# After the last attention head: its scaling moved to ScalarE, two additions moved to GpSimd, two filler products fewer, and the first expert's product placed earlier

## The chip, the cores and the metric

The kernel runs on one core of a Trainium2 chip. The metric is the device time of one execution in microseconds (us), of which the median over several runs counts. TensorE (PE) multiplies, VectorE (DVE) and ScalarE (ACT) work element by element and can read the accumulators in PSUM, GpSimd (POOL) works element by element on SBUF, and SyncE (SP) issues all the transfers of this kernel.

## The reference, cut to what matters

Sixteen heads of hash-bucket attention (768 positions, 64 wide) make 1536 tokens of 512 values; a soft mixture of experts and a gated feed-forward layer follow, all in float32.

```python
mask = q_bucket[:, :, :, None] == k_bucket[:, :, None, :]
scores = np.where(mask, scale * q @ k.T, -1e9)          # per head
attn = softmax(scores);  x = attn @ v                   # x: 1536 x 512, head n fills 64 columns

logits = x @ phi                                        # 1536 x 32 slots, 4 for each of 8 experts
d = softmax over tokens of logits
slot_input = d.T @ x                                    # 32 x 512
h = np.maximum(slot_input[e] @ w1[e], 0)                # w1: 8 x 512 x 1024, 16 MB
slot_out[e] = h @ w2[e]                                 # w2: 8 x 1024 x 512, 16 MB
c = softmax over slots of logits;  y = c @ slot_out     # 1536 x 512

h = y @ w_in;  out = (h * sigmoid(1.702 * h)) @ w_out   # 512 -> 2048 -> 512
```

## The kernel before, in words

**Attention.** A long string, `ATTENTION`, lists every step of the sixteen heads in the order in which each engine's queue receives them; nothing reorders them later. The score steps (`c`, `s`) make a 128 x 384 block of scores, `e` (ScalarE, line 556) takes the exponential into a tile `P`, `av` (TensorE, line 571) multiplies it with the values, and `p` (`psum_add`, line 564) adds up the six `P` tiles of a head into `Ps`, from which `sum1` gets the softmax denominators. For heads 0 to 14 the additions are on GpSimd, for head 15 on VectorE. `Ps` has two halves (`h` 0 and 1) of 384 columns; `p.15.4.1` is head 15's addition of tile 4 into half 1.

**The chain behind the last two heads.** For heads 14 and 15 TensorE sums the columns of `Ps` (line 612), VectorE transposes the sums (line 614), two small operations add the count of positions without a match (lines 628 and 631, on GpSimd for head 14 and on VectorE for head 15), and VectorE takes the reciprocal `rr` (line 633). Head 14 is then scaled by `xnorm1` (step `xg.14`, line 679): six operations of 128 x 64, each with one column of `rr`, from `nv` into the token tiles `XH`. Head 15's product is copied out of PSUM by `avo.15` (ScalarE, line 581), transposed on TensorE (`xtok.15`, line 650) and scaled by six VectorE operations (`xn1.15`, line 729). The string ends with

```
sum1.14 av.15.4 av.15.5 xg.14 avo.15 sum1.15 xtok.15 xn1.15 raw.16
```

**The slots.** Six transposes `xTp` (line 839) take the columns that heads 14 and 15 have filled, two copies into `etile` follow (line 844 on ScalarE, line 842 on VectorE), filler products `spin("t3")` on TensorE (line 203; the table `W` says how many, and their result is not used), and the last part of the logits (line 848). Then come a maximum, exponentials, transposes, and the slot inputs in two halves of 256 columns: `slots(i, t)` multiplies on TensorE (line 887), `slots1(i)` scales on VectorE (line 896), `slots2(i)` transposes on TensorE (line 903) and copies into `siT[i]` on ScalarE (line 904).

**The experts.** `expert_in` multiplies `siT` with the first-layer weights: four tiles of 1 MB to a group, of which `c` = 0 and 1 need `siT[0]`, and 2 and 3 need `siT[1]` (line 1029, result `hp`). Each tile that has been used is given back (`give`), and `more()` then issues the next transfer of the list `coming` into the free place; line 232 is the transfer of a whole 1 MB tile `w`. The list holds `w15` to `w31`, then the weights of the feed-forward layer. `etile` also occupies such a place. The second layer follows on TensorE (line 1068, result `sop`), and behind it the feed-forward layer, whose 384 large products (line 1218) fill TensorE until the end.

Of the kernel before, what the change touches and what calls it, by code (L numbers as in the profile page):

```python
# [8 lines left out]
AF = mybir.ActivationFunctionType  # L9
ALU = mybir.AluOpType  # L10
# [151 lines left out]
def build(nc, tc, qk0, qk, v, phi, consts, w1a, w1, w2, w_in, w_out, out):  # L162
# [4 lines left out]
    V = nc.vector  # L167
    A = nc.scalar
    G = nc.gpsimd
# [15 lines left out]
    def xrow():  # L185
        return XH[:, rows_of.popleft(), :]
# [2 lines left out]

    W = {'s0': 6, 's1': 2, 's2': 1, 's3': 1, 's6': 1, 's7': 3, 's8': 2, 't0': 0, 't1': 0, 't2': 0, 't3': 3, 't4': 2, 't5': 0, 't6': 0, 't7': 0, 'f0': 2, 'f1': 0, 'f2': 4, 'f3': 8, 'f4': 13}
    idle = {}
    bz = cpool.tile([128, 1], F32, name="bz")
    V.memset(LT[:, 0:128], 0.0)
# [2 lines left out]
    def spin(n):  # L198
        spins(W[n])

    def spins(n):
        for _ in range(n):
            T.matmul(idle[0], LT[:, 0:128], LT[:, 0:128], start=True, stop=True)
# [13 lines left out]
    def give(name):  # L217
        free.append(slot_of.pop(name))
# [30 lines left out]
    def piece(w, j):  # L249
        return w[j] if isinstance(w, list) else w[:, j, :]  # L250
# [80 lines left out]
    vsb, Pt, Ps, mxs, xu, rec, xTs, nvs, sms, xtp = {}, {}, {}, {}, {}, {}, {}, {}, {}, {}  # L331
# [226 lines left out]
    def psum_add(n, kt, h):  # L558
        if kt == 1 and h == 0:
            Ps[n] = pq.tile([128, S], F32, name=f"Ps{n}", tag="Ps", bufs=3)  # L560
        last = n == NH - 1
        e = V if last else G
        c = slice(h * HS, (h + 1) * HS)
        e.tensor_tensor(out=Ps[n][:, c], in0=Pt[n, 0][:, c] if kt == 1 else Ps[n][:, c], in1=Pt[n, kt][:, c], op=ALU.add)  # L564

# [86 lines left out]
    def xout(n, i):  # L652
        b, h = n // H, n % H
        return xt[b * 6 + i][:, h * D : (h + 1) * D]
# [21 lines left out]

    def xnorm1(n):
        for i in range(KT):
            G.tensor_scalar(
                out=xout(n, i), in0=nvs[n][:, i, :], scalar1=rec[n][:, i : i + 1], scalar2=None, op0=ALU.mult  # L680
            )

    def xtrans(p, hf):
        b, c = p // 4, p % 4
# [38 lines left out]
    def pool_norm(n):  # L723
        xnorm1(n)
# [16 lines left out]
    def load_phi():  # L741
# [5 lines left out]
        "code": code0, "raw": load_raw, "v": load_v, "win": load_win, "we": load_expert, "wx": lambda k: load_part(NWA, k), "phi": load_phi,  # L747
        "a0": amax0, "a": amax, "mred": mred, "mr0": mrow0, "mr1": mrow1, "mp": mprep, "mr": mrow, "ms": mstore,
        "c": cross, "s": scores, "e": power, "p": psum_add, "av": av, "avo": avout, "vs": vsum, "vs2": vsum2, "sum": sums, "rec": recs,
        "sum1": sums1, "nom": nomatch, "xtok": xtok, "xn": xnorm, "xp": xplus, "xadd": xadd1, "xg": pool_norm, "xn1": norms,  # L750
        "xT": xtrans, "lg": logits, "w1": win1, "w2": win2, "w3": win3, "w4": win4,
# [52 lines left out]
    def more():  # L804
        while coming and free and (coming[0][0] is load_expert or any(x != "wc" for x in free)):
            f, a = coming.popleft()
            f(*a)
# [10 lines left out]
    def mm(shape, name):  # L818
        return mps.tile(shape, F32, name=name, tag="mm", bufs=4)
# [29 lines left out]
    for g in range(4):  # L849
        r = slice(32 * g, 32 * g + 32)  # L850
        G.tensor_copy(
            out=R4[r, :].rearrange("p (r j) -> p r j", r=4), in_=ident[r, r].unsqueeze(1).to_broadcast([32, 4, 32])
# [13 lines left out]
    t1 = mm([128, 128], "cm1")  # L866
# [4 lines left out]
    for t in range(3):  # L871
        t3 = mm([128, 128], f"etp{t}")
# [12 lines left out]
    def slots(i, t):  # L885
        for g in range(4):
            T.matmul(
                sps[i][32 * g : 32 * g + 32, :],
                E[:, t, 32 * g : 32 * g + 32],
                xt[3 * g + t][:, i * 256 : i * 256 + 256],  # L890
                start=t == 0,
                stop=t == 2,
            )

    def slots1(i):
        V.tensor_scalar(
            out=Ssb[i], in0=sps[i], scalar1=fac, scalar2=None, op0=ALU.mult
        )

    def slots2(i):  # L900
        t5 = mm([128, 2, 32], f"sip{i}")
        for c in range(2):
            T.matmul(t5[:, c, :], Ssb[i][:, c * 128 : (c + 1) * 128], I4, start=True, stop=True)
        A.copy(out=siT[i], in_=t5)
# [3 lines left out]
    t2 = mm([128, 1], "cm2")  # L908
# [8 lines left out]
    slots2(0)  # L917
    V.tensor_reduce(out=den, in_=den3, axis=AX.X, op=ALU.add)
    V.tensor_tensor(out=den, in0=den, in1=fac, op=ALU.mult)
    slots(1, 1)  # L920
    slots(1, 2)
    slots1(1)
    t4 = mm([128, 1], "den2")
    T.matmul(t4, R4, den, start=True, stop=True)
    dn1 = col("dn1")
# [97 lines left out]
    def expert_in(g, fh, between=None):  # L1023
        hp = mps.tile([128, 512], F32, name=f"hp{g}{fh}", tag="hp", bufs=2)
        for c in range(4):
            i = (g * 2 + fh) * 4 + c
            w = wtile.pop(i)
            for j in range(4):
                T.matmul(hp[32 * j : 32 * j + 32, :], siT[c // 2][:, c % 2, :], piece(w, j), start=c == 0, stop=c == 3)
            give(f"w{i}")  # L1030
            more()
            if c == 0 and between:
                between()
        hs = xrow()
        V.tensor_scalar(
            out=hs, in0=hp, scalar1=0.0, scalar2=emr[:, g : g + 1], op0=ALU.max, op1=ALU.mult
        )
        return hs

    def expert_tr(g, fh, hs):  # L1040
        tp = mm([128, 4, 128], f"hTp{g}{fh}")
        for t in range(4):
            T.transpose(tp[:, t, :], hs[:, t * 128 : (t + 1) * 128], ident)
        hT[g, fh] = xrow().rearrange("p (t c) -> p t c", t=4)
        A.copy(out=hT[g, fh], in_=tp)

    def last_slots():
        slots2(1)
        give("etile")
        more()  # L1050

    done = []
    for g in range(2):
        for fh in range(2):
            done.append((g, fh, expert_in(g, fh, None if done else last_slots)))

            if len(done) == 3:
                expert_tr(*done[0])
                expert_tr(*done[1])
# [3 lines left out]
    for g in range(2):  # L1063
        for fc in range(8):
            i = 16 + g * 8 + fc
# [12 lines left out]
            for x in early.get(i, "").split():  # L1078
                e, f = x.split(".")
# [265 lines left out]
```

## Time and profile before

| what | value |
|---|---|
| median of 3 runs | 437.98 us (437.12 to 439.15) |
| the profiled execution | 437.46 us |
| its span in the profile | 435.5 us |
| mean granted TensorE clock | 0.999 |
| TensorE busy | 425.6 us, 98% of the span |
| VectorE, ScalarE, GpSimd busy | 303.3, 282.1, 221.5 us |
| transfers | 73.22 MB, mean 168 GB/s |

The profile is one execution; 1.96 us of its time lie outside the span. Times in the rows below count from the start of the span. A busy TensorE here is an engine that has an instruction in flight, so the 98% say little about a single stretch. Between 223 and 298 us the transfers of the expert and feed-forward weights run at 300 to 430 GB/s with one gap; from 300 us on there are next to none.

### The profile page before, as it was taken

How to read it: one execution, taken by the hardware profiler on the slowest of the kernel's cores; microseconds unless marked ns; L12 is line 12 of the kernel's file. 1: busy time of each engine (PE TensorE's matmuls, PEld its weight loads, DVE VectorE, ACT ScalarE, POOL GpSimd, SP SyncE). 2: the span in 40 equal slices, each digit the busy share in tenths (PEclk: the TensorE clock that was granted, in tenths of full speed). 3: DMA queues.
4: the chain of work that ended last, by engine and by line, in shares of the span. 5: the costliest groups of instructions: out<-in, count | busy, mean ns of one | idle time of the engine just before them, and what ended most of it. 6: DMA issues, size and time to landing. Idle time of an engine off the chain costs nothing.

```text
span 435.5 us, 8323 instructions
## 1 busy us (share of the span) xinstructions
PE 425.6 (98%) x2968; PEld 284.7 (65%) x2968; DVE 303.3 (70%) x520; ACT 282.1 (65%) x571; POOL 221.5 (51%) x258
## 2 busy tenths in 40 slices
PE   8999999999999999999999999999999999999996
PEld 6646656566666566656564333577787888888885
DVE  4788798978979899878876226578776845445441
ACT  7668887877889898877862006465776646445441
POOL 5648777888787876979973002234656310000000
PEclk9999999999999999999999999999999999999999
DMA  7454457454557453663799899994000003001001
GB/s 239 132 173 135 127 179 233 150 178 155 171 192 215 130 211 134 210 229 84 263 295 406 335 423 396 417 424 190 1 2 1 2 0 146 0 0 74 0 2 72
DMA packets 28373, 73.22 MB, mean 168 GB/s; under 512 B 4398, under 2 KB 9512, under 8 KB 24876
## 3 DMA queue, kind: packets, MB, share of 16 engines
q1 hardware_dynamic: 28332, 72.69, 47.1%
q8 instruction: 23, 0.38, 0.3%
q14 instruction: 18, 0.15, 0.1%
HBM read 64.16 MB, written 7.34 MB: 164 GB/s over the span
## 4 chain that ended last, share of the span: by engine, by line
PE 76%; DMA 8%; DVE 7%; ACT 5%; issue 1%; SPq 1%; POOL 1%; ACTq 0%; DVEq 0%; POOLq 0%
PE o L1218 30%; PE av L571 12%; PE b L542 8%; PE a L494 7%; PE b L550 7%; DMA w<-in_w 6%; PE h L1190 3%; DVE MX L501 2%; DVE QK L393 1%; SPq L398 1%; ACT QK L371 1%; DVE Ps L564 1%; PE bp L425 1%; PE sm L612 1%; PE xtp L650 1%
## 5 line engine op out<-in xcount | busy, mean ns | idle before, releaser
L564 POOL TENSOR_TENSOR Ps<-Ps,P 128x384 f32<-128x384 f32 x120 | 119.8, 1015 | 9.8 <-ACT P L556 7.4
L1218 PE MATMUL o<-wh,ring 128*128 128x512 f32 x384 | 110.2, 396 | 0.6 <-DVE cT L981 0.6
L556 ACT ACTIVATE P<-b 128x384 f32<-128x384 f32 x192 | 86.8, 488 | 23.0 <-PE b L550 20.3
L501 DVE TENSOR_REDUCE MX<-a 128x1 f32<-128x768 f32 x90 | 85.6, 951 | 19.4 <-PE a L494 18.3
L1218 PEld LDWEIGHTS o<-wh,ring 128*128 128x128 f32 x384 | 71.0, 188 | 15.7 <-issue 1.4
L571 PE MATMUL av<-P,v 128*32 128x384 f32 x768 | 75.5, 492 | 0.0
L1199 DVE TENSOR_TENSOR XH<-h,XH 128x384 f32<-128x384 f32 x64 | 35.3, 556 | 46.4 <-ACT XH L1195 46.3
L542 PE MATMUL b<-QK 128*128 128x384 f32 x192 | 66.7, 369 | 0.4 <-ACT P L556 0.2
L550 PE MATMUL b<-QK 78*128 78x384 f32 (+1 forms) x192 | 60.9, 349 | 0.3 <-ACT QK L531 0.3
L1218 PE MATMUL o<-wl,ring 128*128 128x512 f32 x192 | 55.4, 395 | 0.0
L1195 ACT ACTIVATE XH<-h 128x384 f32<-128x384 f32 x64 | 31.3, 491 | 30.1 <-PE h L1190 30.1
L494 PE MATMUL a<-QK 77*128 77x384 f32 x180 | 50.0, 359 | 0.8 <-DVE MX L501 0.2
L1204 ACT CAST ring<-XH 128x384 fp32r<-128x384 f32 x64 | 32.7, 513 | 23.3 <-DVE XH L1199 22.1
L542 PEld LDWEIGHTS b<-QK 128*128 128x128 f32 x192 | 35.5, 188 | 16.7 <-ACT P L556 8.7
L1218 PEld LDWEIGHTS o<-wl,ring 128*128 128x128 f32 x192 | 35.8, 188 | 10.6 <-issue 2.5
L550 PEld LDWEIGHTS b<-QK 78*128 78x128 f32 (+1 forms) x192 | 35.7, 189 | 6.5 <-issue 5.9
L564 POOL TENSOR_TENSOR Ps<-P,P 128x384 f32<-128x384 f32 x30 | 30.2, 1010 | 19.0 <-ACT P L556 18.9
L494 PEld LDWEIGHTS a<-QK 77*128 77x128 f32 x180 | 29.9, 189 | 13.6 <-DVE MX L501 9.2
L1019 POOL TENSOR_TENSOR wl<-XH,wh 128x512 fp32r<-128x512 f32 x16 | 22.7, 1421 | 31.0 <-ACT wh L1014 30.8
L1209 DVE TENSOR_TENSOR ring<-XH,ring 128x384 fp32r<-128x384 f32 x64 | 37.4, 588 | 1.4 <-ACT ring L1204 1.1
L571 PEld LDWEIGHTS av<-P,v 128*32 128x32 f32 x768 | 19.9, 109 | 23.8 <-issue 21.3
L393 DVE TENSOR_TENSOR QK<-raw,lo 64x384 fp32r<-64x384 f32 x56 | 30.9, 552 | 2.1 <-ACT lo L387 0.9
(171 smaller groups left out, 535.4 us busy)
## 6 DMA issues: line engine op xcount, KB each, us to landing
w<-in_w SPq DMA_DIRECT2D x17, 1024.0 KB
w<-in_w1a SPq DMA_DIRECT2D x56, 256.0 KB
wif<-in_w_in SPq DMA_DIRECT2D x16, 512.0 KB
wof<-in_w_out SPq DMA_DIRECT2D x7, 1024.0 KB
raw<-in_qk SPq DMA_DIRECT2D x15, 384.0 KB
win<-wn SPq DMA_DIRECT2D x16, 256.0 KB
v<-in_v SPq DMA_DIRECT2D x16, 192.0 KB
win<-win SPq DMA_DIRECT2D x3, 1024.0 KB
```

Source lines behind the costliest of these rows:

```text
L393: V.tensor_tensor(out=QK1[n % 2][r, s, c], in0=raw[n][r, c], in1=lot[h][r, :].bitcast(F32), op=ALU.subtract)
L494: T.matmul(a[:, h, 0:HS], q2[0:CROW + 1, 0, i * 128 : (i + 1) * 128], q2[0:CROW + 1, 1, h * HS : (h + 1) * HS], start=True, stop=True,)
L501: V.tensor_reduce(out=MX[:, n % 2, i : i + 1], in_=a[:, :, 0:HS], axis=AX.XY, op=ALU.max)
L542: T.matmul(b, q1[:, 1, kt * 128 : (kt + 1) * 128], q1[:, 0, h * HS : (h + 1) * HS], start=True, stop=False)
L550: T.matmul(b, q2[rows, 1, kt * 128 : (kt + 1) * 128], q2[rows, 0, qs], start=False, stop=True)
L556: A.activation(out=Pt[n, kt][:, h * HS : (h + 1) * HS], in_=bps[n, kt, h], func=AF.Exp, scale=0.125)
L564: e.tensor_tensor(out=Ps[n][:, c], in0=Pt[n, 0][:, c] if kt == 1 else Ps[n][:, c], in1=Pt[n, kt][:, c], op=ALU.add)
L571: T.matmul(avp[n][32 * c : 32 * c + 32, :], vt[n][:, kt, d : d + 32], Pt[n, kt][:, h * HS : (h + 1) * HS], start=kt == 0, stop=kt == KT - 1,)
L1199: V.tensor_tensor(out=gt[i], in0=hp[i], in1=gt[i], op=ALU.mult)
L1204: A.copy(out=gh[i], in_=gt[i])
L1209: (e or V).tensor_tensor(out=gl[i], in0=gt[i], in1=gh[i].bitcast(F32), op=ALU.subtract)
L1218: T.matmul(op[grp, t], u[i][:, t * 128 : (t + 1) * 128], w[wq][:, wi, :], start=f == 0 and j == 0, stop=f == NF - 1 and j == 2,)
```

## The change

It makes four edits. `xnorm1` runs its six operations on ScalarE in place of GpSimd. Of head 15's additions, `p.15.4.1` and `p.15.5.1` go to GpSimd, the other eight stay on VectorE. `spin("t3")` issues one filler product in place of three. The second half's remaining slot products (`slots(1, 1)`, `slots(1, 2)`, `slots1(1)`) leave their place ahead of the first expert and are issued from `expert_in`, behind its first weight tile; `last_slots` moves from behind the first tile to behind the second.

```diff
-    W = {..., 't3': 3, 't4': 2, ...}
+    W = {..., 't3': 1, 't4': 2, ...}
...
         last = n == NH - 1
-        e = V if last else G
+        e = V if last and (h == 0 or kt < 4) else G
...
     def xnorm1(n):
         for i in range(KT):
-            G.tensor_scalar(
-                out=xout(n, i), in0=nvs[n][:, i, :], scalar1=rec[n][:, i : i + 1], scalar2=None, op0=ALU.mult
-            )
+            A.activation(out=xout(n, i), in_=nvs[n][:, i, :], func=AF.Copy, scale=rec[n][:, i : i + 1])
...
     V.tensor_tensor(out=den, in0=den, in1=fac, op=ALU.mult)
-    slots(1, 1)
-    slots(1, 2)
-    slots1(1)
     t4 = mm([128, 1], "den2")
...
             give(f"w{i}")
             more()
-            if c == 0 and between:
-                between()
+            if c < 2 and between:
+                between[c]()
...
+    def more_slots():
+        slots(1, 1)
+        slots(1, 2)
+        slots1(1)
...
-            done.append((g, fh, expert_in(g, fh, None if done else last_slots)))
+            done.append((g, fh, expert_in(g, fh, None if done else (more_slots, last_slots))))
```

Here is ScalarE's queue at the end of attention, before the change; `P_5` are the exponentials of head 15, `xu` is the copy `avo.15`.

```order
L556 ACTIVATE P_3_3181<-b_3_1_3200 128x384
L556 ACTIVATE P_5_3164<-b_5_1_3179 128x384
L581 COPY xu_3265<-av_3212 128x384
L844 COPY etile<-xTp_3329 128x384
L864 ACTIVATE etile,den_3353<-lg,nmx 128x128 x3
```

And here is the same place after the change.

```order
L556 ACTIVATE P_3_3181<-b_3_1_3200 128x384
L556 ACTIVATE P_5_3164<-b_5_1_3179 128x384
L679 ACTIVATE XH<-nv_3193,rr_3249 128x64 x6
L581 COPY xu_3265<-av_3212 128x384
L842 COPY etile<-xTp_3329 128x384
L862 ACTIVATE etile,den_3351<-lg,nmx 128x128 x3
```

Head 14's six scalings now stand ahead of head 15's copy `xu` on the same queue. Below is one piece of the difference of GpSimd's queue at the same place; `nv` is the part of positions without a match, `rec` belongs to head 14.

```order
 L640 TENSOR_TENSOR nv_3177<-vsb_3150,nma 128x384
 L640 TENSOR_TENSOR nv_3193<-vsb_3150,nma 128x384
+L564 TENSOR_TENSOR Ps_3134<-Ps_3134,P_4_3095 128x384
+L564 TENSOR_TENSOR Ps_3134<-Ps_3134,P_5_3164 128x384
 L628 TENSOR_SCALAR rec_3246<-nma 128x6
 L631 TENSOR_TENSOR rec_3246<-sms_3244,rec_3246 128x6
-L679 TENSOR_SCALAR XH<-nv_3193,rr_3249 128x64 x6
```

The two additions stand ahead of both small operations of head 14's denominators. TensorE's queue from the first half's slot transposes (`sip`) on reads so before the change (`sps` are the slot products, `hp` the first expert's):

```order
L903 MATMUL sip_3398<-phs,etile 128x32 x2
L887 MATMUL sps_3375<-XH,etile 32x256 x8
L924 MATMUL den_3413<-den,phs 128x1
L1029 MATMUL hp_3421<-w_137,siT_3372 32x512 x4
L903 MATMUL sip_3428<-phs,etile 128x32 x2
L1029 MATMUL hp_3421<-w_325,siT_3372 32x512 x4
L1029 MATMUL hp_3421<-w_545,siT_3373 32x512 x4
```

And so after the change:

```order
L901 MATMUL sip_3396<-phs,etile 128x32 x2
L919 MATMUL den_3402<-den,phs 128x1
L1024 MATMUL hp_3410<-w_137,siT_3370 32x512 x4
L885 MATMUL sps_3373<-XH,etile 32x256 x8
L1024 MATMUL hp_3410<-w_325,siT_3370 32x512 x4
L901 MATMUL sip_3432<-phs,etile 128x32 x2
L1024 MATMUL hp_3410<-w_545,siT_3371 32x512 x4
```

The first expert's product has passed the eight slot products. The first product that reads the copy of the second half's `sip` (`siT_3373`, now `siT_3371`) had one other weight tile's products between itself and that `sip`; now it stands directly behind it.

## Rows read from the trace of the kernel before

**Rows 1.** Page, part 2: granted TensorE clock in 40 slices of the span.

```profile
PEclk9999999999999999999999999999999999999999
```

**Rows 2.** Chain that ended last, 231 to 274 us: start, length, what.

```profile
231.37 0.20 POOL rec L631
231.91 2.54 POOL XH L679 x6
234.82 0.67 PE idle L203 x6
235.49 0.88 PE lg L848 x4
...
241.78 1.00 PE sps L887 x16
...
243.09 0.99 PE hp L1029 x8
244.09 0.56 PE sip L903 x4
...
255.89 17.51 DMA w<-in_w
```

**Rows 3.** Windows: engines' busy time and instructions, clock, DMA share, GB/s.

```profile
242.00:244.00 2.00, 2.00 (x26) 0.67 (x18) 0.94 (x4) 0.03 (x1) 0.00 (x0) 1.00 0.76 311
244.00:246.00 2.00, 2.00 (x24) 1.04 (x24) 0.00 (x0) 0.21 (x1) 0.00 (x0) 1.00 0.43 98
256.00:260.00 4.00, 4.00 (x44) 1.17 (x36) 0.75 (x1) 0.00 (x0) 0.00 (x0) 1.00 1.01 426
```

**Rows 4.** Timeline of the transfer queue and of TensorE's weight loads.

```profile
244.15 0.33 SPq L232 DMA_DIRECT2D w<-in_w  x1
...
272.15 0.13 PEld L1068 LDWEIGHTS sop<-w,XH 128*32 128x32 f32 x4 [0.30 <-issue]
273.45 0.16 PEld L1068 LDWEIGHTS sop<-w,XH 128*32 128x32 f32 x8 [1.17 <-DMA w<-in_w]
```

**Rows 5.** Additions: timeline of VectorE and GpSimd, then line 564 (min/median/max ns).

```profile
224.40 1.25 DVE L564 TENSOR_TENSOR Ps<-Ps,P 128x384 f32<-128x384 f32 x1
228.25 0.54 DVE L564 TENSOR_TENSOR Ps<-Ps,P 128x384 f32<-128x384 f32 x1
...
224.03 1.21 POOL L564 TENSOR_TENSOR Ps<-Ps,P 128x384 f32<-128x384 f32 x1
...
L564 POOL TENSOR_TENSOR Ps<-Ps,P x120: 992/1010/1377, 19.9 to 224.0; 128x384 f32<-128x384 f32 x120
```

**Rows 6.** Timeline of ScalarE, then line 967.

```profile
231.22 0.48 ACT L581 COPY xu<-av 128x384 f32<-128x384 f32 x1 [3.87 <-PE av L571]
234.47 0.48 ACT L844 COPY etile<-xTp 128x384 f32<-128x384 f32 x1 [2.78 <-POOL XH L679]
236.99 0.37 ACT L864 ACTIVATE etile<-lg,nmx 128x128 f32<-128x128 f32 x1 [2.04 <-DVE nmx L856]
...
244.69 0.21 ACT L904 COPY siT<-sip 128x64 f32<-128x64 f32 x1 [2.66 <-PE sip L903]
...
L967 ACT COPY XH<-XH x8: 272/278/283, 265.8 to 267.0; 128x96 f32<-128x96 f32 x8
```

**Rows 7.** Timeline of VectorE and TensorE, 231 to 236 us.

```profile
231.61 0.19 DVE L633 RECIPROCAL rr<-rec 128x6 f32<-128x6 f32 x1 [0.39 <-POOL rec L631]
232.67 1.24 DVE L729 SCALAR_TENSOR_TENSOR XH<-xtp,rr,nv 128x64 f32<-128x64 f32 x6
234.92 0.56 DVE L842 COPY etile<-xTp 128x384 f32<-128x384 f32 x1 [1.00 <-issue]
...
231.75 0.55 PE L650 MATMUL xtp<-cst,xu 128*128 128x128 f32 x3
```

**Rows 8.** Windows behind the last product, columns as in group 3.

```profile
433.00:434.00 1.00, 0.00 (x0) 0.00 (x0) 0.00 (x0) 0.00 (x0) 0.00 (x0) 1.00 0.76 260
434.00:436.00 2.00, 0.00 (x0) 0.00 (x0) 0.00 (x0) 0.00 (x0) 0.00 (x0) 0.64 0.00 1
```

More of the change, by code (lines that the diff above doesn't have):

```diff
@@ L188, in build @@
     ones = cst[:, C_ONE : C_ONE + 32]
-    W = {'s0': 6, 's1': 2, 's2': 1, 's3': 1, 's6': 1, 's7': 3, 's8': 2, 't0': 0, 't1': 0, 't2': 0, 't3': 3, 't4': 2, 't5': 0, 't6': 0, 't7': 0, 'f0': 2, 'f1': 0, 'f2': 4, 'f3': 8, 'f4': 13}
+    W = {'s0': 6, 's1': 2, 's2': 1, 's3': 1, 's6': 1, 's7': 3, 's8': 2, 't0': 0, 't1': 0, 't2': 0, 't3': 1, 't4': 2, 't5': 0, 't6': 0, 't7': 0, 'f0': 2, 'f1': 0, 'f2': 4, 'f3': 8, 'f4': 13}
     idle = {}
```

## The prediction

> **What bounds the kernel now.** I read the page's line of the granted clock first: TensorE has its full clock in all 40 slices [rows 1], so no stretch is dear because of the clock. Then I read the chain that ended last, from the end backwards, to find what the edited stretch is worth. Behind 274 us it is TensorE's large products; ahead of that the second layer of the experts waits until 273.45 for its last weight tile [rows 4], whose transfer was issued at 255.89 [rows 2]. So the edits, all ahead of 246 us, reach the end of the kernel only through this meeting of two paths: TensorE's own work and the weight transfers.
>
> How near the two paths lie is read from TensorE's weight loads [rows 4]. They come every 0.43 us (0.30 idle and 0.13 load). Behind the one at 272.15 the next was due at 272.58 and came at 273.45. TensorE is thus only 0.87 us ahead of the transfers: a gain on the transfers alone is worth at most 0.87 us, and a delay on TensorE alone is free up to 0.87 us.
>
> The windows [rows 3] show what the transfers lack: at their full rate they move 426 GB/s, but 311 from 242 to 244 us and 98 from 244 to 246. That is 2 x (115 + 328) / 426 = 2.1 us of lost transfer time, because no place was free until the first expert's first tile had been used: its products ran from 243.09 for 0.99 us [rows 2], and the next transfer was issued at 244.15 [rows 4].
>
> What sets 243.09 is the chain behind the last heads, where I read engine by engine: reciprocal of head 14 at 231.61 on VectorE [rows 7], six scalings on GpSimd from 231.91 for 2.54 us [rows 2], transposes, filler products, logits, slots. Beside it runs head 15: copied by ScalarE at 231.22 [rows 6], transposed on TensorE at 231.75, scaled on VectorE from 232.67 for 1.24 us [rows 7], done at 233.91. GpSimd's scalings, done at 234.45, are the later of the two by 0.54 us.
>
> **Two additions on GpSimd.** VectorE loses two additions of 0.54 us, but the sums of head 14 now wait for GpSimd. Head 15's addition 3 into half 1 runs on VectorE from 228.25 for 0.54 us [rows 5]; with the hand-over of 0.11 us that is seen between the reciprocal's end (231.80) and 231.91, GpSimd starts at 228.90. Two additions at the median of 1.01 us [rows 5] end at 230.92. Only then come the two small operations of head 14 at some 0.20 us each [rows 2], and VectorE's reciprocal 0.04 us later: 231.36 against 231.61, a gain of 0.25 us. With the least duration, 0.992, it is 0.29; with the greatest, 1.377, it is a loss of 0.48.
>
> On VectorE the neighbours pay. While GpSimd's addition ran from 224.03 to 225.24, VectorE's addition of the same shape took 1.25 us and ended 0.41 us behind it; alone it took 0.54 [rows 5]. So `p.15.5.0` will end near 229.91 + 0.41 = 230.3, where three additions in a row of 0.54 us would end at 229.9. The transposition of head 14's sums follows before 231.0, when GpSimd is still at its queue: no cost beyond what is counted.
>
> This is what the Trainium skill says against such a move (GPSIMD Engine Reference, Key points): GpSimd shares its SBUF interfaces with VectorE and contends with instructions that have two SBUF inputs. This case's trace agrees (1.25 against 0.54 us); by the rule alone the two additions would be a loss for VectorE, which the sum above allows for.
>
> **Scaling on ScalarE.** The trace has no ScalarE operation of 128 x 64 whose scale is a column of a tile. The nearest are copies of 128 x 96 at 0.278 us, which start 1.2 / 7 = 0.17 us apart, and exponentials of 128 x 128 with a column operand at 0.37 [rows 6]. I take 0.31 us for one and 0.20 from start to start (the overlap of the copies, 0.11, taken off): 5 x 0.20 + 0.31 = 1.3 us for six. The ends are 5 x 0.17 + 0.27 = 1.1 us and, without any overlap, 6 x 0.37 = 2.2 us. So the six fall from 2.54 to 1.3 us.
>
> The Trainium skill prices an ACTIVATE with immediates at 186 ns plus 0.833 ns for each column, 93 more for a column operand, and lets neighbours overlap by 93 (ScalarE: Activation LUTs, What ACT_TABLE_LOAD costs). By it the six would take an estimated 5 x 0.24 + 0.33 = 1.5 us, 0.2 us more than the rows give, and the result would be 0.2 us later.
>
> But in ScalarE's queue the six stand ahead of head 15's copy, which before ran at 231.22 and so ahead of the reciprocal. That copy is what is late next, and TensorE's transposes, VectorE's six scalings and the last transposes wait behind it. Step by step: reciprocal 231.36 + 0.19 + hand-over 0.11 = 231.66; six scalings to 232.96; copy 0.48, to 233.44; transposes 0.05 later and 0.55 long, to 234.04; VectorE's six 0.05 later and 1.24 long, to 235.33. Before, the last scaling ended at 234.45. Head 15, which had 0.54 us to spare, now ends the stretch **0.88 us later** than GpSimd did. From the bounds (additions 0.992 or 1.377, scalings 1.1 or 2.2) this lies between +0.6 and +2.5 us.
>
> **Filler products.** Six records took 0.67 us [rows 2], so four records fewer are 0.45 us. They lay beside VectorE's copy, which ended at 234.92 + 0.56 = 235.48 [rows 7], while ScalarE's had ended at 234.95 [rows 6]. Without them the first half of the logits can run from about 235.0, and the second at 235.53, where before it started about halfway through the 0.88 us from 235.49 [rows 2]. I take 0.3 us of gain; the bounds are 0 and 0.45. Together the stretch ends 0.88 - 0.3 = **0.6 us later** (+0.2 to +2.5).
>
> **First expert first.** Ahead of the first tile's products 1.00 us of slot products goes away [rows 2]; the wait for the first half's copy gives some 0.05 back. The first tile is thus free 0.95 us earlier within this chain. The slot products return behind it, so TensorE's work up to the third tile is the same. But the second half's `sip` now stands directly ahead of the third tile's products, which need ScalarE's copy of it. Before, this copy (244.69, 0.21 us long [rows 6], behind the `sip` that ends at 244.65 [rows 2]) lay beside the second tile's products. Now TensorE waits: 0.04 + 0.21 + 0.05 = 0.3 us, and with the refilling of its pipeline I take 0.4 (0.3 to 0.5). A further place, that of `etile`, comes free only behind the second tile; that is 1.00 + 0.99 + 0.56 = 2.6 us behind the first, but the second tile's own place comes free 2.0 us behind the first, while one transfer of 1.05 MB at 426 GB/s still runs (2.5 us), so the queue need not run dry again.
>
> **The sum.** Transfers: 0.6 - 0.95 = 0.35 us earlier, to 273.10. TensorE: 272.58 + 0.6 + 0.4 = 273.58. The later decides: 273.6 against 273.45, so **+0.1 us**. The profiled execution took 437.46 us (span 435.5 and 1.96 around it), so 437.6 by its own time. It lies 0.5 us below the median of the runs shown; on the median's scale the forecast is 438.1 us. With all bounds (stretch +0.2 to +2.5, wait 0.3 to 0.5) the change is -0.4 to +2.1 us.
>
> **The rivals.** A measurement of this kernel tells some 0.5%, 2.2 us, from no change.
>
> *The early release counts.* If GpSimd's two additions and the six scalings go at their lower ends and the copy of head 15 does not bind as I think, the stretch ends where it did, the transfers gain 0.95 us and TensorE loses 0.4 of its 0.87: -0.5 us, 437.5. The tight spacing of ScalarE's copies speaks for it, the order of its queue against it. For more than 2.2 us the stretch itself would have to end 1.7 us earlier, since TensorE's path then binds; no row offers that much. Chance 0.22, of which 0.04 beyond 2.2 us.
>
> *GpSimd drags.* If both additions take 1.377 us and the six scalings do not overlap, head 15 ends the stretch up to 2.5 us later: +2.1, 440.1. For it speaks that VectorE and GpSimd work against each other there [rows 5], against it that the median of 120 such additions is near their least. Chance 0.12, of which 0.03 beyond 2.2 us.
>
> *The clock falls: slower.* Between the column sums of head 15 and the late transposes TensorE now has nothing to do for some 1.8 us (the transposes that began at 231.75 [rows 7] begin at 233.49), and with fewer fillers little until 236. At the end of the span the clock is still 1.00 from 433 to 434 with no product at all, and 0.64 behind it [rows 8]. If it falls from 2.4 to 1.2 GHz here, each product of the following chain costs double: the rows of logits, slot products, first tile and `sip` alone add 0.88 + 1.00 + 0.99 + 0.56 = 3.4 us on TensorE's path, 441.5. It decides once the fall precedes 237 us. That the clock never fell in the chain before [rows 1] speaks against it. Chance 0.06.
>
> **How the numbers follow.** The forecast, a meeting point within half a microsecond or so of before, has 0.60. The range takes in the bounds, -0.4 to +2.1 us, and the spread of single runs: 436.8 to 440.0 us. Faster by over 0.5%: 0.04; within: 0.87; slower: 0.09.
>
> **What would show it.** In the changed profile: head 14's six on ScalarE in 1.1 to 1.6 us; head 15's copy behind them near 233 and not at 231.2; the last transposes near 235.4; the reciprocal of head 14 between 231.3 and 231.7; the first new weight transfer issued near 243.8; a wait of 0.3 to 0.5 us for `siT` at the third tile; and at the last weight tile no wait, or a short one, where 0.87 us stood. I am wrong if the copy of head 15 is not late, if the gap of the transfers closes by over 1 us, or if the granted clock shows anything below 1.00 between 232 and 246 us.

## The result and the profile after

The changed kernel takes 440.85 us (median of 20 executions, 439.19 to 443.96), the kernel before, on the same chip, 438.75 us (20 executions, 436.89 to 443.85). The ratio is 1.0052, with a 95% interval of 1.0035 to 1.0068: the kernel became slower by some 2.2 us. The forecast was 438.1 us and its range ended at 440.0. The profiled execution took 442.58 us, with a span of 440.6.

The page of the changed kernel shows the granted clock of TensorE in 40 slices of the span. Before, no slice was below 9 [rows 1].

```profile
PEclk9999999999999999999996999999999999999999
```

One slice, from 231 to 242 us, shows a 6. The windows of the changed kernel around it (window, length, busy us and instructions of PE, PEld, DVE, ACT and POOL, granted clock, DMA share, GB/s) say where it begins and ends.

```profile
233.50:234.00 0.50, 0.00 (x0) 0.00 (x0) 0.19 (x1) 0.50 (x4) 0.00 (x0) 1.00 0.75 311
234.00:234.50 0.50, 0.00 (x0) 0.00 (x0) 0.00 (x0) 0.50 (x4) 0.00 (x0) 0.97 1.75 344
234.50:235.00 0.50, 0.07 (x1) 0.07 (x2) 0.00 (x0) 0.37 (x2) 0.00 (x0) 0.50 0.51 213
...
240.50:241.00 0.50, 0.50 (x3) 0.14 (x1) 0.03 (x1) 0.00 (x0) 0.00 (x0) 0.50 1.05 442
241.00:241.50 0.50, 0.50 (x4) 0.50 (x4) 0.50 (x1) 0.00 (x0) 0.46 (x2) 0.70 0.93 393
241.50:242.00 0.50, 0.41 (x4) 0.16 (x2) 0.18 (x2) 0.43 (x3) 0.42 (x3) 1.00 1.05 442
```

From about 234.5 to 241.3 us TensorE had 0.50 of its clock, 1.2 in place of 2.4 GHz, although it was busy again from 234.93. What it did before the fall is in the timeline of the changed kernel (start, length, engine, line, operation; in brackets the idle time ahead and what ended it).

```profile
229.67 1.19 POOL L564 TENSOR_TENSOR Ps<-Ps,P 128x384 f32<-128x384 f32 x1 [1.49 <-DVE Ps L564]
230.94 1.20 POOL L564 TENSOR_TENSOR Ps<-Ps,P 128x384 f32<-128x384 f32 x1
232.22 0.21 POOL L628 TENSOR_SCALAR rec<-nma 128x6 f32<-128x6 f32 x1
232.51 0.20 POOL L631 TENSOR_TENSOR rec<-sms,rec 128x6 f32<-128x6 f32 x1
...
232.75 0.19 DVE L633 RECIPROCAL rr<-rec 128x6 f32<-128x6 f32 x1 [0.91 <-POOL rec L631]
235.87 1.24 DVE L727 SCALAR_TENSOR_TENSOR XH<-xtp,rr,nv 128x64 f32<-128x64 f32 x6 [2.18 <-PE xtp L650]
...
232.97 1.54 ACT L679 ACTIVATE XH<-nv,rr 128x64 f32<-128x64 f32 x6 [4.90 <-DVE rr L633]
234.42 0.45 ACT L581 COPY xu<-av 128x384 f32<-128x384 f32 x1
...
232.19 0.53 PE L612 MATMUL sm<-Ps,cst 128*32 128x192 f32 x8 [0.37 <-POOL Ps L564]
234.93 0.90 PE L650 MATMUL xtp<-cst,xu 128*128 128x128 f32 x3 [2.20 <-ACT xu L581]
235.76 1.51 PE L825 MATMUL lg<-LT,cst 128*32 128x192 f32 x16
```

Read from the bottom: TensorE's transposes of head 15 wait 2.20 us for ScalarE's copy `xu`; the copy stands behind the six scalings; these waited 4.90 us for VectorE's reciprocal; and the reciprocal waited for GpSimd's small operations, which stand behind the two additions. Then the clock falls, and the transposes take 0.90 us where they took 0.55 [rows 7].

The two profiles are shifted against each other by work that the edits don't touch, so I compare starts counted from one of VectorE's operations that both have, head 14's sum `nv<-xtp,nv` of line 675 (at 227.78 before, 228.52 after). I call these counted starts.

| kernel | reciprocal, head 14 | copy, head 15 | maximum `nmx` | first new transfer | end of experts, `c4p` |
|---|---|---|---|---|---|
| before | 3.83 | 3.44 | 8.62 | 16.37 | 46.73 |
| after | 4.23 | 5.90 | 12.45 | 19.26 | 50.39 |

The kernel loses 3.66 us in this execution between the attention and the end of the experts. Its span is 5.1 us longer; of the rest 0.74 us lie ahead of the operation counted from, where the edits touch nothing, and 0.7 behind `c4p`, which comes up again under the order alone. Not every execution loses that: of the 20, 11 show a mean granted clock of 1.000 (median 439.65 us), 5 show 0.996 (441.27 to 441.52), and 4, with the profiled one, 0.991 (442.58 to 443.96).

At the last weight tile, where TensorE waited before [rows 4], its loads now wait 0.35 us in place of the usual 0.30:

```profile
277.02 0.13 PEld L1068 LDWEIGHTS sop<-w,XH 128*32 128x32 f32 x4 [0.30 <-issue]
277.50 0.13 PEld L1068 LDWEIGHTS sop<-w,XH 128*32 128x32 f32 x4 [0.35 <-DMA w<-in_w]
```

### The profile page after: what moved, and what is told of

Its sections match the earlier page's. It is cut to its first block, busy times and chain, and to the rows that moved or that the text cites. A ratio compares the mean times of both kernels' runs of the same rounds, so it can differ in the third digit from the quotient of the medians.

```text
span 440.6 us, 8310 instructions
## 1 busy us (share of the span) xinstructions
PE 428.7 (97%) x2964; PEld 285.9 (65%) x2964; DVE 302.6 (69%) x518; ACT 283.4 (64%) x577; POOL 220.8 (50%) x254
## 5 line engine op out<-in xcount | busy, mean ns | idle before, releaser
L564 POOL TENSOR_TENSOR Ps<-Ps,P 128x384 f32<-128x384 f32 x122 | 122.1, 1016 | 11.5 <-ACT P L556 7.4
```

## The experiments

My theory after the result: the order of ScalarE's queue delays head 15, and the gap that this leaves on TensorE lowers the clock, so that one delay is paid twice. The rivals: the additions on GpSimd do it; the new order at the first expert does it, since TensorE's path now binds; or the gap only costs its length.

### The copy ahead of the scalings

In the order that is written out by hand, `avo.15` goes ahead of `xg.14`; all else is as in the changed kernel. It was run twice.

```diff
-p.15.5.1 sum1.14 av.15.4 av.15.5 xg.14 avo.15 sum1.15 xtok.15 xn1.15 raw.16
+p.15.5.1 sum1.14 av.15.4 av.15.5 avo.15 xg.14 sum1.15 xtok.15 xn1.15 raw.16
```

> The changed kernel, with head 15's copy out of PSUM put ahead of head 14's six scalings in ScalarE's queue, nothing else. Theory 1 (the copy behind the scalings makes a gap of 2.7 us on TensorE, and in that gap the granted clock falls): the copy starts near 232 us in place of 234.4, no TensorE gap over 1.2 us is left, the granted clock stays at 1.00, and the time is 1 to 2.5 us below the changed kernel, a ratio to the kernel before of 0.999 to 1.003. Theory 2 (the two additions on GpSimd are what makes the chain late): the last transposes move by under 0.5 us and the ratio stays at 1.004 or more. Theory 3 (the new order at the first expert costs the time): ratio unchanged at 1.005.

Measured: 439.56 us, ratio 1.0026 (1.0005 to 1.0048), with executions from 437.63 to 442.86. Timeline of this kernel:

```profile
231.07 0.48 ACT L581 COPY xu<-av 128x384 f32<-128x384 f32 x1 [3.87 <-PE av L571]
232.10 1.54 ACT L679 ACTIVATE XH<-nv,rr 128x64 f32<-128x64 f32 x6 [0.55 <-DVE rr L633]
...
231.78 0.55 PE L650 MATMUL xtp<-cst,xu 128*128 128x128 f32 x3
```

The copy is back at a counted start of 3.43, TensorE's gap is gone (it was 2.20 us; the 2.7 of the expectation count the column sums in), and `nmx` (8.50) and `c4p` (46.65) stand where they stood before. The profile and the median disagree: the upper executions reach above 440 us at a full clock as well as at 0.996. So the same kernel ran again on another chip.

> The changed kernel with head 15's copy ahead of head 14's scalings, once more, since its executions fell into a group of 437.6 to 438.1 us and a tail up to 442.9 with clocks that did not explain it. If the tail is that of every kernel here (the kernel before has executions from 436.7 to 442.9 too): ratio 0.998 to 1.002 with most executions near 438. If the additions on GpSimd make it: ratio 1.002 to 1.004 again, with executions above 440 in a third.

Measured: 438.40 us, ratio 0.9998 (0.9977 to 1.0019), no execution above 439.52, `c4p` at 46.44. The upper executions of the first run did not come back, and what made them is open. By the profiles of both runs the loss up to `c4p` is gone once the copy has its old place, and by the median of the second the whole; the first run's interval leaves room for up to half of one per cent.

### The additions back on VectorE

Only the additions are undone; the copy still stands behind the scalings.

```diff
-        e = V if last and (h == 0 or kt < 4) else G
+        e = V if last else G
```

> The changed kernel, with all ten additions of head 15 on VectorE again; scaling on ScalarE, one filler, and the new order stay. Theory 1: the reciprocal of head 14 comes 0.4 to 0.7 us earlier (two additions on GpSimd took 2.46 us in the changed kernel), the gap on TensorE shrinks from 2.2 to some 1.7 us but is still there, so the clock still falls in some executions; ratio 1.002 to 1.005. Theory 2: the chain is back where it was before and the ratio is 0.998 to 1.001. Theory 3: ratio 1.005.

Measured: 440.94 us, ratio 1.0049 (1.0031 to 1.0067), as slow as the changed kernel. Six of 10 executions show a clock of 0.995 or 0.996 (440.88 to 441.88 us), four 1.000 (439.05 to 439.82), the profiled one among these. Its timeline:

```profile
231.77 1.54 ACT L679 ACTIVATE XH<-nv,rr 128x64 f32<-128x64 f32 x6 [4.49 <-DVE rr L633]
233.22 0.46 ACT L581 COPY xu<-av 128x384 f32<-128x384 f32 x1
...
233.73 0.55 PE L650 MATMUL xtp<-cst,xu 128*128 128x128 f32 x3 [2.18 <-ACT xu L581]
```

Without the additions the gap is still 2.18 us and not the 1.7 expected, and at a full clock `c4p` comes at 47.74, 1.01 us later than before. So the additions alone are not the cause.

### The gap filled

Nine filler products are put between head 15's column sums and its transposes. The chain is as late as in the changed kernel, but TensorE is busy.

```diff
-... xg.14 avo.15 sum1.15 xtok.15 xn1.15 raw.16
+... xg.14 avo.15 sum1.15 idle2.0 spin.9 xtok.15 xn1.15 raw.16
...
+    def idle2(k):
+        idle[0] = pps.tile([128, 128], F32, name="idle_gap", tag="A", bufs=1)
```

> The changed kernel with nine filler products of 128 x 128 on TensorE between the column sums of head 15 and its transposes, some 2.0 us of work in the gap, with a result that is not used. Theory 1: the granted clock is 1.00 in every execution; the part of the loss that is the clock goes and the part that is the later chain stays, so the ratio is 1.001 to 1.003, and no execution is more than 2 us above the least. Rival (the clock's fall is no matter, since the transfers decide the end): ratio 1.005 as for the changed kernel, clock or not.

Measured: 440.01 us, ratio 1.0032 (1.0018 to 1.0046), all 12 executions at 0.998 or above and none above 440.98. The chain that ended last in this kernel (start, length, what), and its windows:

```profile
232.42 2.20 PE idle_gap L203 x18
...
234.62 0.55 PE xtp L650 x3
235.17 0.79 PE lg L828 x16
...
237.22 1.18 PE lg L849 x3
```

```profile
234.00:236.00 2.00, 2.00 (x26) 1.27 (x25) 0.79 (x5) 0.57 (x2) 0.00 (x0) 1.00 0.94 365
236.00:241.00 5.00, 4.51 (x28) 2.26 (x28) 2.63 (x10) 1.90 (x8) 1.14 (x4) 1.00 1.01 423
```

The same pieces in the changed kernel's chain (of the last, four products stand in this chain and three in the other):

```profile
234.93 0.90 PE xtp L650 x3
235.83 1.44 PE lg L825 x16
...
239.17 1.77 PE lg L846 x4
```

The clock stays at 1.00, and `nmx` starts at 10.19 in place of 12.45: in the profiled execution the fallen clock cost 2.26 us. What is left is the delay itself: `nmx` 1.57 us and `c4p` 1.40 us later than before (48.13 against 46.73). So the gap is what lowers the clock, and the loss has both parts. That rests on the profile and on the clocks, none of 12 below 0.998 against 9 of 20; the ratios alone don't show it, since the two intervals overlap (the changed kernel's begins at 1.0035).

The same fillers with the additions back on VectorE (the two edits above together):

> The changed kernel with all additions on VectorE again and nine filler products in TensorE's gap, so that of the head's two delays only the copy behind the scalings is left, at full clock. Theory 1: TensorE's second expert layer ends 1.0 us later than in the kernel before, as in the kernel with the additions back (there 1.01 us by the traces, but with clocks of 0.995 to 0.996 in 6 of 10 executions); ratio 1.001 to 1.003, clock 0.998 or more in every execution. Rival (the clock of 0.996 in those executions had another cause than the gap): clocks of 0.996 or less again in a third or more, ratio 1.004 or more.

Measured: 440.32 us, ratio 1.0037 (1.0019 to 1.0055), `nmx` at 9.80, `c4p` at 47.73, 1.00 us later than before; 10 of 11 executions at 0.998 or above. The interval reaches down into what was expected, its middle lies above it. With a full clock, all the edits but the additions thus cost 1.0 us at `c4p`. The place of the copy makes more than that: with the copy first and the additions on VectorE `c4p` comes at 46.03 (below), 1.70 us earlier.

### One edit alone, on the kernel before

First the additions only:

> The kernel before with only the two additions moved to GpSimd. Theory 1: each addition takes 1.2 us beside VectorE, the reciprocal of head 14 comes 0.6 to 0.7 us later and GpSimd's six scalings with it, so the last transposes are 0.6 us later; TensorE's slack of 0.87 us at the last weight tile takes none of it, since the transfers are later too; ratio 1.000 to 1.003. Rival (the additions are free, as the prediction had it): ratio 0.998 to 1.000 and the reciprocal where it was.

Measured: 438.99 us, ratio 1.0014 (0.9986 to 1.0043). Timeline:

```profile
229.20 2.46 POOL L564 TENSOR_TENSOR Ps<-Ps,P 128x384 f32<-128x384 f32 x2 [1.49 <-DVE Ps L564]
...
232.28 0.19 DVE L633 RECIPROCAL rr<-rec 128x6 f32<-128x6 f32 x1 [0.91 <-POOL rec L631]
```

The reciprocal comes at 4.23, 0.40 us later than before and not 0.6 to 0.7, `nmx` 0.38 later, and `c4p` only 0.18, where the expectation saw nothing absorbed.

Then `t3` at 1 only:

> The kernel before with only the two filler products fewer. Theory 1: the logits end 0.2 to 0.3 us earlier, no gap on TensorE grows beyond 0.6 us, clock unchanged; ratio 0.998 to 1.001. Rival (the fillers keep the clock up): clocks of 0.996 or less in a third or more of the executions and a ratio of 1.003 or more.

Measured: 437.98 us, ratio 0.9987 (0.9964 to 1.0009). Timeline:

```profile
235.69 1.36 PE L848 MATMUL lg<-etile,phs 128*32 128x384 f32 x4
...
235.60 0.56 DVE L842 COPY etile<-xTp 128x384 f32<-128x384 f32 x1 [1.00 <-issue]
237.09 0.56 DVE L856 TENSOR_REDUCE nmx<-lg 128x1 f32<-128x384 f32 x1 [0.93 <-PE lg L848]
```

The logits stretch from 0.94 to 1.36 us, since their second half waits for VectorE's copy, and `nmx` starts at 8.61 against 8.62: the fillers lay entirely beside that copy.

Then the order at the first expert only:

> The kernel before with only the new order at the first expert: the second half's slot products behind the first weight tile, its transposes behind the second. Theory 1: it costs nothing or gains little, the transfers start 0.9 us earlier, TensorE waits some 0.4 us for the second half's copy; ratio 0.998 to 1.001. Theory 3 (the new order is the loss): ratio 1.003 to 1.006, and the wait of TensorE for the copy, or a longer gap in the transfers, shows it.

Measured: 439.12 us, ratio 1.0005 (0.9987 to 1.0024). Timeline of SP and TensorE, and the chain:

```profile
243.40 2.69 SPq L232 DMA_DIRECT2D w<-in_w  x3
...
244.99 0.63 PE L903 MATMUL sip<-phs,etile 128*128 128x32 f32 x4
245.92 1.06 PE L1026 MATMUL hp<-w,siT 128*32 128x512 f32 x8 [0.30 <-ACT siT L904]
```

```profile
262.38 12.15 PE sop L1070 x112
```

The first transfer starts at 15.42 against 16.37, 0.95 us earlier; the third tile waits for `siT` and starts 0.26 us later (17.95 against 17.68 counted); and the second layer's 112 products run without the wait at the last tile. Yet `c4p` comes only 0.18 us earlier. Why is in these rows, from TensorE's timeline of the kernel before:

```profile
272.57 0.61 PE L1068 MATMUL sop<-w,XH 128*32 128x512 f32 x4
273.45 1.07 PE L1068 MATMUL sop<-w,XH 128*32 128x512 f32 x8 [0.26 <-DMA w<-in_w]
```

There the weight loads had waited 1.17 us, 0.87 beyond the usual [rows 4]. The products start 0.88 us behind the four ahead of them, where 0.43 is usual (112 in 12.15 us, four at a time), so they lost only 0.45: the loads run ahead of them. The step behind a wait is longer too, 0.45 us. In all TensorE had 0.47 us to win, less 0.29 for the new wait.

And the products behind the experts are slower. Here are the large products of the feed-forward layer (min/median/max ns, first and last start) and the last piece of the chain, first in the kernel before, then with the new order:

```profile
L1218 PE MATMUL o<-wh,ring x384: 388/393/793, 280.7 to 431.4; 128*128 128x512 f32 x192
423.61 8.20 PE o L1218 x36
...
L1220 PE MATMUL o<-wh,ring x384: 387/394/793, 280.7 to 432.1; 128*128 128x512 f32 x192
424.13 8.33 PE o L1220 x36
```

The first starts at the same time and the last 0.64 us later. There is no new wait: no single product falls behind by more than 0.014 us. It is so in all eight profiles of the seven kernels that have the new order as the change has it, where the 384 products take 151.35 to 151.39 us from the first start to the last; in the five profiles of the others it is 150.72 to 150.74. So the new order gains 0.18 us at `c4p` and loses 0.45 at the last product, which the interval of its time neither shows nor excludes. What makes the products slower is open. In the seven the place of `etile` is given back behind the second tile's, in the others ahead of it, so that later weights come to lie in other places; whether that is the cause no run shows.

### Both costly edits undone, and a version with an earlier slot

The copy goes first and the additions stay on VectorE (both diffs above); what is left are the scalings on ScalarE, the fillers and the new order.

> The changed kernel with both suspects undone: all ten additions on VectorE, and head 15's copy ahead of head 14's six scalings, which stay on ScalarE; one filler and the new order stay. Theory 1 (the copy behind the scalings, and to a lesser part the additions on GpSimd, make the loss): the six end near 233.3 us, the last transposes near 234.1, 0.4 us ahead of the kernel before; granted clock 0.998 or more; ratio 0.996 to 1.000. Rival (the new order or the missing fillers carry a part of the loss): ratio 1.002 or more.

Measured: 438.52 us, ratio 0.9986 (0.9960 to 1.0012), `nmx` at 8.10 and `c4p` at 46.03, 0.70 us earlier than before in the profile, but the last product only 0.05 earlier (203.58 against 203.63 counted), since the new order slows the large products. In the next kernel `last_slots` is called in the middle of the second tile's products, so that the copy `siT` lies beside the other half:

```diff
+                if c == 1 and j == 1 and between:
+                    between[1]()
...
-            if c < 2 and between:
-                between[c]()
+            if c == 0 and between:
+                between[0]()
```

> The kernel with both suspects undone (additions on VectorE, copy first), and in addition the second half's four slot transposes placed in the middle of the second weight tile's products in place of behind them, so that ScalarE's copy lies beside two pieces of that tile. Theory 1: TensorE's wait for that copy, 0.3 us, goes, and the third tile's products start 0.2 to 0.4 us earlier; where the transfers meet TensorE this gives 0 to 0.4 us; ratio 0.995 to 0.999. Rival: VectorE's scaling of the second half is not ready at that place and TensorE waits for it as long; ratio as without the split.

Measured: 438.24 us, ratio 0.9982 (0.9959 to 1.0005), `c4p` at 46.50. Its timeline shows the `sip` products behind four products of the tile; the wait for `siT` is shorter, but the weight loads of `sip` now wait 0.84 us for VectorE's scaling `etile`, as the rival had it: the third tile starts no earlier and `c4p` comes 0.47 us later than in the kernel above. What it wins it wins behind: its large products take 150.73 us again, and the last comes at 203.40, 0.18 earlier.

```profile
243.49 1.03 PE L1024 MATMUL hp<-w,siT 128*32 128x512 f32 x4
244.45 0.63 PE L901 MATMUL sip<-phs,etile 128*128 128x32 f32 x4
...
244.44 0.52 PEld L901 LDWEIGHTS sip<-phs,etile 128*128 128x128 f32 x4 [0.84 <-DVE etile L894]
```

Both are faster than the changed kernel; neither can be told from the kernel before.

### The old order with the gap filled

The changed kernel with the fillers in the gap and the slots back ahead of the first expert: is the new order worth something once the chain is late?

> The changed kernel with the gap filled and the old order at the first expert. Theory 1: the head's delay of 1.4 to 1.6 us now stands in front of the transfers as well, and TensorE waits for the last weight tile again by 0.6 to 0.9 us; ratio 1.003 to 1.005, no less than with the new order (1.0032). Rival (the new order loses time here): ratio 1.002 or less.

Measured: 439.56 us, ratio 1.0018 (0.9994 to 1.0041), `c4p` at 48.23 against 48.13 with the new order. The interval overlaps that of the gap filled with the new order (1.0018 to 1.0046), so by the times it is unclear. In the profiles the new order loses: its last product comes at 205.68 counted, with the old order at 205.15, though with the old one `c4p` is 0.10 us later.

## Why the prediction was wrong

**The clock** is about half of the loss, and it took the time out of the range: the 11 executions at a full clock have a median of 439.65 us, below the range's end. It was the rival that had a chance of 0.06 and no term in the sum, and the clock below 1.00 ahead of 246 us is one of the prediction's own signs of being wrong. The step that failed is the reading of [rows 8]: a clock of 1.00 behind the last product, and never a fall before [rows 1], were taken for evidence that a gap of 1.8 us is harmless. The rows are true of their place: at 434 the clock is still full 2.2 us behind the last product, whose chain ends at 431.81, and only then it falls. Ahead of the transposes it fell 1.8 us behind the column sums (232.19 and 0.53). A gap at one place did not price a gap at another.

The gap came out at 2.20 us, in the changed kernel behind another of 0.37, and the mean clock lay below 0.998 in 9 of 20 executions, and in 6 of 10 with the additions undone. With the gap filled (three kernels) it did so in 2 of 34, with the copy first (four runs) in 3 of 47, in the kernel before, run beside the experiments, in 5 of 96: a few falls belong to every kernel, falls in half of the executions only to the gap. Against the median of the 11 at a full clock the five at 0.996 lie about 1.8 us higher and the four at 0.991 about 3.7. The place named, ahead of 237 us, was right; the rival's 441.5 us is what the five take, and too little for the four. Spread over 20 executions this is (5 x 1.8 + 4 x 3.7) / 20 = 1.2 us.

**The stretch** was forecast 0.6 us later and was 1.57 (`nmx`, gap filled), inside the stated bounds of 0.2 to 2.5. Three terms make up the difference.

- *Reciprocal: -0.25 forecast, +0.40 measured.* The working took the median of 120 additions, 1.01 us. The fitting row was the one beside VectorE's own addition, 1.21 us [rows 5]: the two took 1.19 and 1.20, GpSimd's first began at 229.67, 0.14 us behind the end of VectorE's addition 3 (228.99 and 0.54), and the small operations followed 0.29 us apart, not 0.20. It costs 0.65 us more than forecast, and goes the way of the rival *GpSimd drags*, which had 0.12.
- *Scalings: 1.3 forecast, 1.54 measured.* This line of the changed kernel (min/median/max ns) has the single duration:

```profile
L679 ACT ACTIVATE XH<-nv,rr x6: 331/332/348, 233.0 to 234.2; 128x64 f32<-128x64 f32 x6
```

  They start 0.24 us apart. The estimate of 1.5 us by the Trainium skill (ScalarE: Activation LUTs, What ACT_TABLE_LOAD costs) was nearer than my value from the copies of [rows 6]. From the reciprocal's start to the copy's start it makes 1.67 us against 1.60, only 0.07 more, since the six start 0.22 us behind the reciprocal and not 0.30, and the copy overlaps the last of them.
- *Fillers: -0.3 forecast, 0.0 measured.* The bound of 0 was right, because VectorE's copy sets the second half of the logits.

Together 0.6 + 0.65 + 0.07 + 0.3 = 1.62 us against 1.57 measured. The mechanism itself, head 15's copy caught behind the scalings, was right: its start moved from 3.44 to 5.90.

**The join at the last weight tile** was right in kind: the transfers gain, TensorE's path then binds. Its size was read from the wrong row. I took the wait of the weight loads, 0.87 us beyond the usual, for TensorE's slack; the products had 0.47. With that, TensorE's end moves by -0.47 + 1.57 + 0.29 (the new wait) = 1.39 us; measured 1.40. Against the +0.13 of the sum the slack makes 0.40, the stretch 0.97, and the new wait, forecast at 0.4, takes 0.11 back.

**Behind the join** the sum had nothing: it let the edits reach the end only through that meeting. The new order makes the large products 0.64 us longer, more than it gains ahead of them.

**The range** did not hold what it was said to take in: 437.98 + 2.1 = 440.1 is already above 440.0, with nothing left for the spread of single runs.

**Right** were the 0.95 us of the new order, nearly the wait for `siT` (0.26 to 0.29 us in the order alone, just under the stated 0.3 to 0.5), the absent wait at the last tile, and VectorE's slowed `p.15.5.0`: in the changed kernel the addition beside GpSimd took 1.25 us.

```profile
228.99 0.54 DVE L564 TENSOR_TENSOR Ps<-Ps,P 128x384 f32<-128x384 f32 x1
230.03 1.25 DVE L564 TENSOR_TENSOR Ps<-Ps,P 128x384 f32<-128x384 f32 x1
```

So the loss has three parts. At a full clock `c4p` comes 1.40 us later: with the copy first and without the additions the other edits bring it 0.70 us earlier, the copy's place costs 1.70 (46.03 to 47.73), the additions 0.40 (to 48.13). Behind `c4p` the new order costs 0.64 us. The halved clock adds 1.2 us on the mean. That is 3.2 us, more than the 2.2 measured and just beyond the interval of 1.5 to 3.0. The executions give the delay less than the profiles do: those at a full clock lie 0.9 us above the median of the kernel before (439.65 against 438.75), the gap-filled kernel 0.8 to 2.0 by its interval. That each part is there is shown; its share of the 2.2 us is known only so far.

**Open** is why the clock falls in only about half of the executions of one program, why it falls in a few of the kernels without the gap, why executions at a full clock reach 440 to 442 us in several kernels, the kernel before among them (442.40 us at 1.000), and by what the new order slows the large products. A little of that spread lies ahead of the edits: the operation counted from starts anywhere between 227.64 and 228.96 us in the thirteen profiles. The scalings on ScalarE were not tried by themselves on the kernel before. Where in the span the clock fell in executions that were not profiled is not seen; that filling the gap makes the falls rare speaks for this place.

## What to carry to other kernels

When work moves to another engine, look at what stands behind it in that engine's queue and at when its own input arrives: here six scalings that waited 4.90 us held up a copy that was ready, and putting the copy ahead of them took the loss away by one run and halved it by the other. A delay that leaves TensorE idle in the middle of a dense stretch can cost more than its length, so fill it or avoid it. Price an operation by the row in which its neighbours were as busy as they will be, and read TensorE's slack from the starts of its products, not from the wait of its weight loads. Compare the whole kernel, not the edited stretch alone: an order changed ahead of 250 us made products behind 280 us slower.

## What the runs showed of the hardware

- Behind a gap of about 2.2 us between products the granted clock fell to 0.50 in the profiled execution and stayed there for some 6.8 us, although TensorE was busy again 0.5 us after the fall. The mean clock was below 0.998 in 9 of 20 and 6 of 10 executions of the two kernels with this gap, and 1.00 in the others; with the gap filled it was below in 2 of 34.
- GpSimd and VectorE slow each other in both directions: GpSimd's additions of 128 x 384 took 1.19 and 1.20 us where VectorE was adding too, against a median of 1.01, VectorE's 1.25 against 0.54.
- Weight loads can wait longer than the products behind them: at one tile 0.87 us beyond the usual, where the products started 0.45 us late.
- The same 384 large products took 151.35 to 151.39 us in the eight profiles with the new order at the first expert and 150.72 to 150.74 in the five without it or with the slots placed earlier.
